# Second sweep: value products of four batches at once, with the high and low weight parts stacked in the 128 rows

## The chip, the cores and the metric

The kernel runs on one core of a Trainium2 chip. Five engines work on it, each through its own queue in program order: TensorE (PE, with its weight loads as PEld), VectorE (DVE), ScalarE (ACT), GpSimd (POOL) and SyncE (SP), which issues all DMAs. The metric is the device time of one execution in microseconds. For the kernel before there are three timed runs, 905.22, 906.84 and 908.5 us, with a median of 906.84.

## The reference

Per batch (8) and head (8), with a sequence of 576, a head size of 64 and 32 memory slots:

```python
a = exp(phi - max_s(phi)); a = a / (sum_s(a) + 1e-09)
k_m = einsum('bhsm,bhsd->bhmd', a, k)
v_m = einsum('bhsm,bhsd->bhmd', a, v)
attn = softmax(q @ k_m.T / 8)            # 576 x 32
x = attn @ v_m                           # heads side by side: 4608 x 512
xn = x / sqrt(mean(x*x) + 1e-06) * rms_g
g = xn @ w_gate; val = xn @ w_val        # 512 -> 1536
out = (silu(g) * val) @ w_out            # 1536 -> 512
```

All data is float32. x is never needed as such: attn @ v_m @ W equals attn @ (v_m W), and v_m has only 32 rows per head. The kernel multiplies the small v_m with a slice of the weights first (the "value product") and attn with that result afterwards.

## The kernel before, in words

**Precision.** The large products run in the faster fp32r format. Each float32 operand is split into a high part (a cast to fp32r, on ACT) and a low part (the remainder, by a subtraction on POOL or DVE). A product is high x high + high x low + low x high, so three matmuls.

**Two sweeps.** The eight batches are four pairs. The first part (up to about 150 us) makes k_m and v_m of all batches and the attention of pairs 0 and 1. Then 48 steps follow: steps 0 to 23 are the first sweep, for pairs 0 and 1, steps 24 to 47 the second, for pairs 2 and 3. The 1536 columns are 12 slices of 128; a step is one pair with one slice. Function `where` gives the order: pair A with slices 0 and 1, pair B with slices 0 and 1, and so on. During the first sweep the attention of pairs 2 and 3 is made on the side, and the weights are converted, split and stored in DRAM (`w_dram`, `o_dram`); the second sweep reloads them (`reload`, L439). Slice numbers 12 to 23 are the second sweep's.

**One step.** `vw_steps` makes the value product: `vp`, two halves cc of six matmuls with 256 columns (L854). The 128 rows that are summed over are the 64 dimensions of two heads; the stationary operand `vm` holds those two heads' memory slots in blocks with zeros between them, which were put there when v_m was transposed, for both batches of the pair. The three matmuls per group are (vh, wh), (vh, wl), (vl, wh). `evac` copies the result to `xh` (ACT cast, L867) and `xl` (DVE, L868), 64 rows at a time. `gv_steps` multiplies these with the attention, `ath` and `atl`, into gate and value, `pg` and `pv` (L892), 48 matmuls of 256 or 320 columns, applies silu (ACT, L900) and the product `hf` (DVE, L901), and splits it into `hh` and `hl` (L914, L915). After two steps of a pair, `out_steps` multiplies both with `w_out` (`oh`, `ol`) into `po`, nine tiles of six 512-wide matmuls (L934), and adds them to `acc` (DVE, L942). The last one of a pair writes `acc` to the output (L946, two DMAs of 64 rows per tile).

**The second sweep's values.** `late_vm` (called at the times LV) reloads the value tiles of pairs 2 and 3 from `vg_dram` and splits them, one pair after the other, into the two `vm` buffers.

**What sets the order.** Every piece is entered in a list with a time in units of steps (the table PRM: GV, VW, O, LV, PSW and others). The list is sorted and a scheduler, which simulates the engines, fixes each engine's queue from it. Tiles rotate through a fixed number of buffers per tag, and a writer waits until the old tile's readers are done. PSUM has one buffer for the value product, two each for gate, value and `o`.

Of the kernel before, what the change touches and what calls it, by code (L numbers as in the profile page):

```python
# [8 lines left out]
F32 = mybir.dt.float32  # L9
F32R = mybir.dt.float32r  # L10
# [9 lines left out]
WB = 4  # L20
# [48 lines left out]
    XN=[0.012, 0.176, 0.184, 0.33, 0.33, 0.566, 0.596, 0.699, 0.766],  # L69
    LV=[22.571, 24.198],  # L70
    CB=1,
# [20 lines left out]
def kernel(  # L92
# [43 lines left out]
    make_identity(nc, ident)  # L136
    vm = {}
    gram = {}
# [16 lines left out]
    def split_v(b, vg):  # L155
        pr, j = divmod(b, 2)
        for e in range(2):
            o = e ^ j
            src = vg.rearrange("p (c e) m -> p c e m", e=2)[:, :, o, :]
            hi, lo = vm[pr][:, 0, :, e, o, :], vm[pr][:, 1, :, e, o, :]  # L160
            nc.scalar.copy(hi, src)
            nc.gpsimd.tensor_tensor(out=lo, in0=src, in1=hi.bitcast(F32), op=ALU.subtract)
# [179 lines left out]
    def convert(kind, n):  # L342
# [99 lines left out]
    with ExitStack() as c1:  # L442
# [133 lines left out]
        def kv_steps(b):  # L576
# [59 lines left out]
            def post2():  # L636
                tp = st.pop(("kvt", b))
                km = km_late.get(b)
                if km is None:
                    km = sb.tile([P, HP, 64], F32, tag="km", name=f"km{b}", bufs=4)  # L640
                nc.scalar.copy(km, tp[:, 0])
                st["km", b] = km
                vt = sb.tile([P, HP, 64], F32, tag="vt", name=f"vt{b}")
                nc.scalar.copy(vt, tp[:, 1])
# [184 lines left out]
    NS = (NP // G) * NU * G * 2  # L829
    vw, hsplit, accs = {}, {}, {}  # L830

    def where(i):

        ps_, r = divmod(i, NU * G * 2)
        u, r = divmod(r, G * 2)
        pi, f = divmod(r, 2)
        return ps_, u, ps_ * G + pi, 2 * u + f

    def vw_steps(i):
# [3 lines left out]
        def mm(cc):  # L843
            def f():
                if cc == 0:
                    vw[i] = [ps.tile([P, 2, 2, 256], F32, tag="vw", name=f"vp{i}", bufs=1)]
                vp = vw[i][0]
                vh, vl = vm[pr][:, 0], vm[pr][:, 1]
# [11 lines left out]
        def evac():  # L860
            vp = vw[i][0]
            xh = sb.tile([P, 2, 2, 256], F32R, tag="xh", name=f"xh{i}", bufs=2)
            xl = sb.tile([P, 2, 2, 256], F32R, tag="xl", name=f"xl{i}", bufs=2)
            for h in range(2):
# [5 lines left out]
                ).ins)  # L870
            vw[i] = xh, xl
        return [mm(0), mm(1), evac]

    def gv_steps(i):
        ps_, u, pr, j = where(i)
        steps = []
        for gi, (t0, n) in enumerate(GROUPS):
            N = 64 * n
            for b in range(2):
                def f(gi=gi, t0=t0, n=n, N=N, b=b):  # L880
# [7 lines left out]
                    for half, pt in ((0, pg), (1, pv)):  # L888
                        m = 0
                        for l, r in ((xh, ah), (xh, al), (xl, ah)):  # L890
                            for cc in range(2):
                                nc.tensor.matmul(  # L892
                                    pt[:, :N],
                                    l[:, cc, b, half * P:half * P + P],
                                    r[:, b, cc, t0:t0 + n, :].rearrange("p t x -> p (t x)"),
# [12 lines left out]

            def split(gi=gi, n=n):
                hf = hsplit[i, gi][0]  # L910
                hh = sb.tile([P, n, P], F32R, tag=f"hh{gi}", name=f"hh{i}_{gi}", bufs=3)
                hl = sb.tile([P, n, P], F32R, tag=f"hl{gi}", name=f"hl{i}_{gi}", bufs=3)
                hv = hf.rearrange("p t b x -> p t (b x)")
# [6 lines left out]
    def out_steps(i):  # L920
# [34 lines left out]

    def late_vm(pr):
        new_vm(pr)
        vg = sb.tile([P, 2, HP, 64], F32, tag="vgl", name=f"vgl{pr}")
        for j in range(2):
            nc.sync.dma_start(vg[:, j], vg_dram[2 * pr + j])  # L960
            split_v(2 * pr + j, vg[:, j])

# [97 lines left out]
    for i in range(NS):  # L1060
        ps_, u, pr, j = where(i)
        ev += place(i, PRM["GV"], gv_steps(i))
        if i + 1 < NS:
# [9 lines left out]
    items, again = [x for x in items if x[1] < NJ], [x for x in items if x[1] >= NJ]  # L1073
    for kind, n, p, e in again:
        if kind != 1:
            ev.append((e, lambda kind=kind, n=n: reload(kind, n)))
    for a, (kind, n, p, e) in enumerate(items):
# [8 lines left out]
    for a in range(NP - G):  # L1086
# [3 lines left out]
        ev += place(PRM["XM"][a], PRM["XN"], steps[n:])  # L1090
        ev.append((PRM["LV"][a], lambda a=a: late_vm(G + a)))
    for _, f in sorted(ev, key=lambda e: e[0]):
# [31 lines left out]
```

## Time and profile before

| | |
|---|---|
| timed runs, median (lowest, highest) | 906.84 us (905.22, 908.5) |
| profiled execution, first to last instruction (span) | 901.6 us |
| PE busy | 838.0 us, 93% of the span |
| DVE, ACT, POOL busy | 573.3, 420.6, 328.0 us |
| mean granted TensorE clock | 0.970 |
| DMA queue of SP | 81432 packets, 105.41 MB, 37.5% of 16 engines |
| matmuls | 6207 |

The profile gives the execution's span and no separate time for it; it is set against the timed median, 5.2 us longer. A row of the page's group list names the line, engine, operation, output and inputs, shapes and count, then busy time and the mean of one, then idle time of the engine before them and what ended it. Matmuls overlap, so their mean duration is longer than the distance between two. In a timeline row the first number is the start, the second the time from there to the end of the merged instructions. "SPq" is SP's DMA queue.

### The profile page before, as it was taken

To read this page: it belongs to the slowest core of one execution; us is meant where nothing else is said; L and a number is where in the kernel's file an instruction comes from. 1 tells how busy PE (TensorE), PEld (TensorE's weight loads), DVE (VectorE), ACT (ScalarE), POOL (GpSimd) and SP (SyncE) were. 2 spreads that over 40 slices of the span, in tenths; PEclk is the share of its full clock that TensorE was granted. 3 is DMA by queue.
4 is the path that set the end of the run, shared out by engine and by line. 5 is a ranking of instruction groups with operands and counts; after the bars stand their busy time and mean duration, and the time that the engine had idled before them with its cause. 6 is when DMAs were issued, how large, how long until landed. Compare 5 with 4: busy or idle time off the path is not lost.

```text
span 901.6 us, 15803 instructions
## 1 busy us (share of the span) xinstructions
PE 838.0 (93%) x6207; PEld 744.9 (83%) x6207; DVE 573.3 (64%) x994; ACT 420.6 (47%) x717; POOL 328.0 (36%) x274
## 2 busy tenths in 40 slices
PE   4999487999998999998999999899999999999997
PEld 4777476888887898987888897898899999999996
DVE  5578956877569878787877746522445455454543
ACT  2657334777745655655544532344423333333330
POOL 3564735563634543633533531411212111121120
PEclk9889787999999999999999999999999999999999
DMA  8976554354325433443333343501204012040046
GB/s 285 341 250 232 202 167 128 108 164 121 126 68 157 148 96 104 151 135 113 128 105 110 103 109 106 129 9 53 88 1 141 1 48 94 1 141 1 1 115 142
DMA packets 81506, 106.41 MB, mean 118 GB/s; under 512 B 34324, under 2 KB 52248, under 8 KB 81432
## 3 DMA queue, kind: packets, MB, share of 16 engines
q1 hardware_dynamic: 81432, 105.41, 37.5%
q8 instruction: 49, 0.80, 0.4%
q14 instruction: 25, 0.20, 0.1%
HBM read 73.93 MB, written 31.46 MB: 117 GB/s over the span
## 4 chain that ended last, share of the span: by engine, by line
PE 70%; DVE 13%; issue 5%; DMA 5%; POOL 3%; ACT 3%; SPq 1%; POOLq 0%; DVEq 0%; ACTq 0%
PE po L934 28%; PE pv L892 14%; PE pg L892 13%; PE vp L854 7%; PE kvp L587 3%; DMA phi<-in_phi_dram 2%; DVE xl L868 1%; POOL w L399 1%; DMA kv<-in_v_dram 1%; DVE ex L353 1%; DVE acc L942 1%; PE xp L236 1%; POOL hl L915 1%; ACT xh L867 1%; PE S L1000 1%
## 5 line engine op out<-in xcount | busy, mean ns | idle before, releaser
L915 POOL TENSOR_TENSOR hl<-hf,hh 128x512 fp32r<-128x512 f32 (+1 forms) x96 | 140.3, 1462 | 356.0 <-ACT hh L914 348.3
L942 DVE TENSOR_TENSOR acc<-po,acc 128x512 f32<-128x512 f32 x180 | 122.4, 686 | 111.2 <-PE po L934 110.3
L934 PE MATMUL po<-oh,hh 128*128 128x512 f32 x432 | 173.3, 402 | 6.9 <-DMA oh<-od 1.6
L934 PE MATMUL po<-oh,hl 128*128 128x512 f32 x432 | 171.4, 397 | 0.0
L934 PE MATMUL po<-ol,hh 128*128 128x512 f32 x432 | 171.1, 396 | 0.0
L868 DVE TENSOR_TENSOR xl<-vp,xh 64x1024 fp32r<-64x1024 f32 x96 | 117.1, 1220 | 55.6 <-ACT xh L867 54.4
L900 ACT ACTIVATE sg<-pg 128x256 f32<-128x256 f32 x192 | 77.2, 409 | 141.4 <-PE pg L892 138.0
L901 DVE TENSOR_TENSOR hf<-pv,sg 128x256 f32<-128x256 f32 x192 | 85.5, 452 | 79.2 <-PE pv L892 51.5
L867 ACT CAST xh<-vp 64x1024 fp32r<-64x1024 f32 x96 | 96.7, 1008 | 51.7 <-PE vp L854 36.0
L914 ACT CAST hh<-hf 128x512 fp32r<-128x512 f32 (+1 forms) x96 | 64.6, 673 | 82.8 <-DVE hf L901 69.9
L934 PEld LDWEIGHTS po<-oh,hh 128*128 128x128 f32 x432 | 81.7, 190 | 21.5 <-DVE acc L942 2.3
L934 PEld LDWEIGHTS po<-oh,hl 128*128 128x128 f32 x432 | 81.7, 189 | 19.6
L934 PEld LDWEIGHTS po<-ol,hh 128*128 128x128 f32 x432 | 81.8, 189 | 11.4
L892 PE MATMUL pg<-ath,xh 128*128 128x320 f32 (+1 forms) x384 | 86.3, 300 | 4.8 <-ACT xh L867 3.6
L854 PE MATMUL vp<-wh,vm 128*128 128x256 f32 x384 | 85.2, 289 | 3.8 <-DVE xl L868 1.7
L892 PE MATMUL pv<-ath,xh 128*128 128x320 f32 (+1 forms) x384 | 85.0, 298 | 0.7 <-DVE hf L901 0.7
L892 PE MATMUL pv<-atl,xh 128*128 128x320 f32 (+1 forms) x384 | 84.8, 296 | 0.0
L892 PE MATMUL pg<-ath,xl 128*128 128x320 f32 (+1 forms) x384 | 84.6, 295 | 0.0
L892 PE MATMUL pg<-atl,xh 128*128 128x320 f32 (+1 forms) x384 | 84.5, 296 | 0.0
L892 PE MATMUL pv<-ath,xl 128*128 128x320 f32 (+1 forms) x384 | 83.0, 295 | 0.0
L892 PEld LDWEIGHTS pg<-ath,xh 128*128 128x128 f32 x384 | 63.5, 189 | 10.6 <-ACT xh L867 4.5
L854 PEld LDWEIGHTS vp<-wh,vm 128*128 128x128 f32 x384 | 65.9, 193 | 7.5 <-ACT wh L416 1.8
(129 smaller groups left out, 1395.2 us busy)
## 6 DMA issues: line engine op xcount, KB each, us to landing
kv<-in_k_dram SPq DMA_DIRECT2D x32, 288.0 KB, 4.7
kv<-in_v_dram SPq DMA_DIRECT2D x32, 288.0 KB, 5.8
out_dram<-acc SPq DMA_DIRECT2D x72, 128.0 KB, 2.4
raw<-in_moe_w_gate_dram SPq DMA_DIRECT2D x12, 512.0 KB, 4.0
raw<-in_moe_w_val_dram SPq DMA_DIRECT2D x12, 512.0 KB, 4.2
wd<-wh SPq DMA_DIRECT2D x12, 512.0 KB, 3.4
wd<-wl SPq DMA_DIRECT2D x12, 512.0 KB, 3.4
raw<-in_moe_w_out_dram SPq DMA_DIRECT2D x12, 512.0 KB, 3.8
```

What stands on the lines that cost most here:

```text
L236: nc.tensor.matmul(xp[64 * j:64 * j + 64, P * cc:P * cc + P], st["at"][:, t, cc, 64 * j:64 * j + 64], gb[:, j, cc], start=True, stop=True,)
L587: nc.tensor.matmul(kvp[64 * par:64 * par + 64, cc, 0:128], e_bd[j][:, hp, c, :], st["kv", b, hp][:, :, 64 * c:64 * c + 64], start=(c == 0) ...
L854: nc.tensor.matmul(vp[:, cc, e, :], lhs(l), r[:, 2 * cc + e, :], start=(n == 0), stop=(n == 2),)
L867: nc.scalar.copy(xh[rows], src)
L868: urgent.append(nc.vector.tensor_tensor(out=xl[rows], in0=src, in1=xh[rows].bitcast(F32), op=ALU.subtract).ins)
L892: nc.tensor.matmul(pt[:, :N], l[:, cc, b, half * P:half * P + P], r[:, b, cc, t0:t0 + n, :].rearrange("p t x -> p (t x)"), start=(m == 0), ...
L900: nc.scalar.activation(sg[:, :N], pg[:, :N], AF.Silu)
L901: urgent.append(nc.vector.tensor_tensor(out=hf[:, :, b, :], in0=pv[:, :N].rearrange("p (t x) -> p t x", x=64), in1=sg[:, :N].rearrange("p ...
L914: nc.scalar.copy(hh, hv)
L915: nc.gpsimd.tensor_tensor(out=hl, in0=hv, in1=hh.bitcast(F32), op=ALU.subtract)
L934: nc.tensor.matmul(po, l[:, tt, :], r, start=(m == 0), stop=(m == 5))
L942: nc.vector.tensor_tensor(out=accs[key], in0=po, in1=accs[key], op=ALU.add).ins
```

## The change

Only the second sweep's value products change, and what feeds them.

- *Rows.* The stored weights are laid out so that, for one head, rows 0 to 63 are one part (high or low) of its 64 rows and rows 64 to 127 the other (the first sweep writes them with four DMAs of 64 rows per slice, before two of 128).
- *Values.* Two tiles `va0` (high) and `va1` (low) take the place of the two pairs' `vm` buffers. Each holds the values of all four batches, once in rows 0 to 63 and once in rows 64 to 127, so that 128 columns are 4 batches x 32 slots of one head. They are fetched by 16 DMAs of 64 rows (`fetch_v`, in the order already at the start of the first sweep), before 4 of 128 rows, and split by `late_v`.
- *Products.* `unit_steps(n)`: for one slice and one head two matmuls, va0 and va1 against the stacked weights, which give all four products of parts. A slice has 8 heads, so 16 matmuls, which serve both pairs.
- *Placing.* The product has its rows in order of batch, the gate products need them in order of head for one batch. ACT and DVE copy the product into staging tiles `sh` (high) and `sl` (low), in buffers that the weight conversion used before. DMAs from SBUF to SBUF, 32 rows each, then put the pieces into `xh` and `xl` of the two steps: 16 for a step, 32 for a slice. The order of heads in the values is permuted (`spread_v`, and `put` in the first part) so that each piece stays in its rows.
- *Order.* From step 28 on the pairs alternate at every step (`mixed`), output groups come after the third and fourth of four steps, and a fourth pair of `hh`/`hl` buffers (`hx`) is added; every third step's `xh`/`xl` are four smaller tiles in another tag. The times U, RL, RW and LV are new.

```diff
-    LV=[22.571, 24.198],
+    LV=[21.0, 21.1, 22.22, 22.25],
+    U=[
+        [-1.6, -1.45, -1.4, -1.25, -0.99, -0.7],
+        [-1.6, -1.5, -1.3, -1.2, -0.99, -0.98],
+        [-1.6, -1.5, -1.3, -1.2, -0.99, 0.01],
+    ],
+    RL=[-2.85, -3.4, -3.3],
+    RW=[1.73, 1.6],
...
+    def spread_v(b, vg):
+        j, pi = b % 2, swapped(b)
+        for h in range(2):
+            x = 4 * h + (h ^ pi)
+            src = vg[:, h].rearrange("p (c e) m -> p c e m", e=2)
+            if j:
+                src = src[:, :, ::-1]
+            places = slice(x + 2, x + 9, 6) if j else slice(x, x + 11, 10)
+            hi, lo = (t[:, :, places, :] for t in vall)
             nc.scalar.copy(hi, src)
             nc.gpsimd.tensor_tensor(out=lo, in0=src, in1=hi.bitcast(F32), op=ALU.subtract)
...
                 for a, t in enumerate(wsplit[n]):
-                    nc.sync.dma_start(w_dram[n][:, a], t.bitcast(F32))
+                    for h in range(2):
+                        r = 64 * (h ^ a)
+                        nc.sync.dma_start(w_dram[n][r:r + 64, h], t[64 * h:64 * h + 64].bitcast(F32))
...
+    def mixed(i):
+        return i >= NS // 2 + 2 * G
...
+        if mixed(i):
+            pi, f = f, pi
...
+    def slot(i):
+        if i >= NS // 2 and i % 3 == 2:
+            t = [[sb.tile([P, 2, 256], F32R, tag="w2", name=f"{x}{i}_{c}", bufs=WB) for c in range(2)] for x in ("xh", "xl")]
+        else:
+            whole[i] = [sb.tile([P, 2, 2, 256], F32R, tag=x, name=f"{x}{i}", bufs=2) for x in ("xh", "xl")]
+            t = [[x[:, c] for c in range(2)] for x in whole[i]]
...
+    def unit_steps(n):
...
+        def mm(cc):
+            def f():
+                st[cc] = vp = ps.tile([P, 2, 2, 256], F32, tag="vw", name=f"vq{n}_{cc}", bufs=1)
+                for e in range(2):
+                    for h in range(2):
+                        k = 8 * e + 4 * h
+                        w = wsplit[n][h][:, 2 * cc + e].rearrange("p g f -> p (g f)")
+                        for a in range(2):
+                            nc.tensor.matmul(
+                                vp[:, h, e, :], vall[a][:, cc, k:k + 4, :].rearrange("p q m -> p (q m)"), w,
+                                start=(a == 0), stop=(a == 1),
+                            )
...
+                for h in range(2):
+                    src = st[cc][:, h]
+                    xh, xl = (x[h][cc] for x in st["x"])
+                    nc.scalar.copy(xh, src)
+                    urgent.append(nc.vector.tensor_tensor(
+                        out=xl, in0=src, in1=xh.bitcast(F32), op=ALU.subtract
+                    ).ins)
...
+        def send(pi):
+            def f():
+                i = steps[pi]
+                slot(i)
+                for a in range(2):
+                    for g in range(4):
+                        rows = slice(32 * g, 32 * g + 32)
+                        for c in range(2):
+                            x = st["x"][a][(g & 1) ^ pi][c][rows].bitcast(F32)
+                            nc.sync.dma_start(vw[i][a][c][rows].bitcast(F32), x[:, ::-1] if g >> 1 else x)
+            return f
+        return [mm(0), take(0), mm(1), take(1), send(0), send(1)]
...
-                for s in (i - 1, i):
+                for s in (i - 2 if mixed(i) else i - 1, i):
...
-        if i % 2:
+        if i % 4 > 1 if mixed(i) else i % 2:
             ev += place(i + 1, PRM["O"], out_steps(i))
+    for n in range(NJ, 2 * NJ):
+        late_n = min(n - NJ, 2)
+        ev += place(steps_of(n)[0], PRM["U"][late_n], unit_steps(n))
+        ev.append((2 * n + PRM["RL"][late_n], lambda n=n: reload(0, n)))
+        ev.append((2 * (n - n % 2) + PRM["RW"][late_n > 1] + 0.1 * (n % 2), lambda n=n: reload(2, n)))
```

More of the change, by code (lines that the diff above doesn't have):

```diff
@@ L640, in post2, with put @@
                     km = sb.tile([P, HP, 64], F32, tag="km", name=f"km{b}", bufs=4)
-                nc.scalar.copy(km, tp[:, 0])
+                def put(dst, src):
+                    if swapped(b):
+                        dst, src = (x.rearrange("p s (h m) -> p s h m", h=2) for x in (dst, src))
+                        src = src[:, :, ::-1]
+                    nc.scalar.copy(dst, src)
+                put(km, tp[:, 0])
                 st["km", b] = km
                 vt = sb.tile([P, HP, 64], F32, tag="vt", name=f"vt{b}")
-                nc.scalar.copy(vt, tp[:, 1])
+                put(vt, tp[:, 1])
                 st["vt", b] = vt, tp
@@ new lines, in steps_of, with take, f @@
+    def steps_of(n):
+        return [i for i in range(NS) if where(i)[0] * NJ + where(i)[3] == n]
+    def unit_steps(n):
+        steps = steps_of(n)
+        st = {}
+        def mm(cc):
[11 more added lines that the diff above has]
+            return f
+        def take(cc):
+            def f():
+                if cc == 0:
+                    high = [wp[0].tile([P, 2, 2, 256], F32R, tag="raw", name=f"sh{n}_{h}", bufs=2) for h in range(2)]
+                    st["x"] = [[[x[:, c] for c in range(2)] for x in high], [[], []]]
+                for h, (pool, tag) in enumerate(((wp[0], "mi"), (sb, "vgl")) if cc else ((wp[0], "ex"), (wp[0], "w"))):
+                    st["x"][1][h].append(pool.tile([P, 2, 256], F32R, tag=tag, name=f"sl{n}_{h}{cc}"))
+                for h in range(2):
[5 more added lines that the diff above has]
+                    ).ins)
+            return f
+        def send(pi):
+            def f():
+                i = steps[pi]
[6 more added lines that the diff above has]
+                            nc.sync.dma_start(vw[i][a][c][rows].bitcast(F32), x[:, ::-1] if g >> 1 else x)
+            return f
+        return [mm(0), take(0), mm(1), take(1), send(0), send(1)]
@@ L907, in gv_steps, with split @@
                 steps.append(f)
-            def split(gi=gi, n=n):
+            def split(gi=gi, t0=t0, n=n):
                 hf = hsplit[i, gi][0]
-                hh = sb.tile([P, n, P], F32R, tag=f"hh{gi}", name=f"hh{i}_{gi}", bufs=3)
-                hl = sb.tile([P, n, P], F32R, tag=f"hl{gi}", name=f"hl{i}_{gi}", bufs=3)
+                if mixed(i) and i % 4 == 3:
+                    if gi == 0:
+                        fourth.append(persist.tile([P, 2, NT, P], F32R, tag="at", name=f"hx{i}"))
+                    hh, hl = (fourth[-1][:, a, t0:t0 + n] for a in range(2))
+                else:
+                    hh = sb.tile([P, n, P], F32R, tag=f"hh{gi}", name=f"hh{i}_{gi}", bufs=3)
+                    hl = sb.tile([P, n, P], F32R, tag=f"hl{gi}", name=f"hl{i}_{gi}", bufs=3)
                 hv = hf.rearrange("p t b x -> p t (b x)")
@@ L954, in o_tile, with fetch_v, late_v @@
         return ps.tile([P, 512], F32, tag="o", name=name)
[L956 to L961, printed above, removed]
+    late = {}
+    def fetch_v(pr):
+        pool, tag = ((sb, "vgl"), (wp[0], "w"))[pr - G]
+        late[pr] = both = pool.tile([P, 2, 2, HP, 32], F32, tag=tag, name=f"vgl{pr}")
+        for k in range(2):
+            b = 2 * pr + k
+            for h in range(2):
+                x = 32 * (h ^ swapped(b))
+                for r in range(2):
+                    nc.sync.dma_start(
+                        both[64 * r:64 * r + 64, k, h], vg_dram[b][64 * h:64 * h + 64, :, x:x + 32]
+                    )
+    def late_v(pr):
+        if not vall:
+            vall[:] = [persist.tile([P, 2, 16, 32], F32R, tag=f"vm{a}", name=f"va{a}") for a in range(2)]
+        both = late.pop(pr)
+        for k in range(2):
+            spread_v(2 * pr + k, both[:, k])
     def attend_steps(pr, s):
@@ L1072 @@
                 items.append((kind, n, 2 * n0 + PRM["PRE" if n0 else "PRE0"][a], 2 * n0 + PRM["PSW"][a]))
[L1073 to L1076, printed above, removed]
+    items = [x for x in items if x[1] < NJ]
     for a, (kind, n, p, e) in enumerate(items):
@@ L1090 @@
         ev += place(PRM["XM"][a], PRM["XN"], steps[n:])
-        ev.append((PRM["LV"][a], lambda a=a: late_vm(G + a)))
+        for p, f in zip(PRM["LV"][a::2], (fetch_v, late_v)):
+            ev.append((p, lambda a=a, f=f: f(G + a)))
     for _, f in sorted(ev, key=lambda e: e[0]):
```

24 lines of the change are left out of this document (14 added, 10 removed).

## The prediction

> **What bounds the kernel now.** I read the totals by engine first, then the stretch of the second sweep in one row, then what TensorE (PE) waits for from 500 us on.
>
> ```profile
> PE 838.0 (93%) x6207; PEld 744.9 (83%) x6207; DVE 573.3 (64%) x994; ACT 420.6 (47%) x717; POOL 328.0 (36%) x274
> core 0: us, PE busy (x) PEld busy (x) DVE busy (x) ACT busy (x) POOL busy (x), PEclk, DMA share, GB/s
> 650.00:850.00 200.00, 200.00 (x1237) 182.21 (x1235) 102.66 (x150) 68.70 (x113) 40.09 (x28) 1.00 0.15 48
> PE rp L205 <- DVE rinv L277: 2.3, 1, 2.3
> PE po L934 <- DMA oh<-od: 1.6, 1, 1.6
> ```
>
> PE is busy for 200 of 200 us, at a granted clock of 1.00, while VectorE (DVE) is half idle and the DMA engines are used at 0.15. After 500 us only two PE waits exceed a microsecond. So here a matmul less is time less, and new time can only come from a wait put in front of PE. The mean of one matmul on the page overlaps its neighbours; the price is the distance between starts:
>
> ```profile
> 713.20 0.46 PE L892 MATMUL pv<-atl,xh 128*128 128x320 f32 x2
> 713.49 0.46 PE L892 MATMUL pv<-ath,xl 128*128 128x320 f32 x2
> 713.78 0.28 PE L854 MATMUL vp<-wh,vm 128*128 128x256 f32 x1
> 713.90 0.29 PE L854 MATMUL vp<-wl,vm 128*128 128x256 f32 x1
> 714.03 0.40 PE L854 MATMUL vp<-wh,vm 128*128 128x256 f32 x2
> 714.27 0.28 PE L854 MATMUL vp<-wl,vm 128*128 128x256 f32 x1
> 714.38 0.28 PE L854 MATMUL vp<-wh,vm 128*128 128x256 f32 x1
> 714.50 0.46 PE L892 MATMUL pg<-ath,xh 128*128 128x320 f32 x2
> 694.12 1.87 PE po L934 x8
> 709.97 1.41 PE po L934 x6
> 750.29 1.87 PE po L934 x8
> ```
>
> Six product matmuls take 714.50 - 713.78 = 0.72 us, 0.12 each; a 320-wide one 0.147 (0.29 for two); a 512-wide one 1.87 / 8 = 0.234. From 694.12 to 750.29 the program repeats itself after four steps, 14.04 us a step.
>
> **Fewer matmuls.** Before, a half of a step's product is six matmuls for one pair of batches:
>
> ```order
> L854 MATMUL vp36_7818<-wh18_7709,vm2_5938 128x256
> L854 MATMUL vp36_7818<-wl18_7710,vm2_5938 128x256
> L854 MATMUL vp36_7818<-wh18_7709,vm2_5938 128x256 x2
> L854 MATMUL vp36_7818<-wl18_7710,vm2_5938 128x256
> L854 MATMUL vp36_7818<-wh18_7709,vm2_5938 128x256
> ```
>
> Now, at the same place on PE, a half is eight, and serves both pairs (vq18 stands for weight slice 18, va0 and va1 for the high and low part of all four batches' values):
>
> ```order
> L898 MATMUL vq18_1_8024<-wh18_7755,va0_5922 128x256
> L898 MATMUL vq18_1_8024<-wh18_7755,va1_5923 128x256
> L898 MATMUL vq18_1_8024<-wl18_7756,va0_5922 128x256
> L898 MATMUL vq18_1_8024<-wl18_7756,va1_5923 128x256
> L898 MATMUL vq18_1_8024<-wh18_7755,va0_5922 128x256
> L898 MATMUL vq18_1_8024<-wh18_7755,va1_5923 128x256
> L898 MATMUL vq18_1_8024<-wl18_7756,va0_5922 128x256
> L898 MATMUL vq18_1_8024<-wl18_7756,va1_5923 128x256
> ```
>
> Per slice that is 16 for 24; over 12 slices 96 matmuls fewer, of the same size: **-96 x 0.12 = -11.5 us**. A slice's two steps go from 28.1 to 27.1 us.
>
> **Evacuation.** Two casts and two subtractions of 64x1024 per step become, per slice, four and four of 128x512.
>
> ```profile
> 710.45 0.62 ACT L914 CAST hh<-hf 128x512 fp32r<-128x512 f32 x1 [1.31 <-DVE hf L901]
> 706.62 1.01 ACT L867 CAST xh<-vp 64x1024 fp32r<-64x1024 f32 x1 [1.01 <-DVE xl L868]
> 711.42 0.69 DVE L942 TENSOR_TENSOR acc<-po,acc 128x512 f32<-128x512 f32 x1 [1.05 <-PE po L934]
> 708.68 1.23 DVE L868 TENSOR_TENSOR xl<-vp,xh 64x1024 fp32r<-64x1024 f32 x1
> ```
>
> By the nearest rows ScalarE (ACT) saves 0.4 and DVE 0.5 us each time. Neither is what PE waits for, so this counts 0.
>
> **The sends** are the new thing between a product and its reader: 32 DMAs of 32 rows (64 KB) per slice, all on SP's queue, 384 in all. The nearest rows are the output writes (64 rows, 128 KB, in a burst at the end) and the od reload:
>
> ```profile
> L946 SPq DMA_DIRECT2D out_dram<-acc x28: 466/594/1347, 875.0 to 898.2; - x28
> DMA to landing us min/median/max: 2.2/2.4/3.6
> 880.38 18.45 SPq L946 DMA_DIRECT2D out_dram<-acc x24
> 743.68 0.86 SPq L439 DMA_DIRECT2D oh<-od x2
> ```
>
> A send should cost SP between 0.43 (0.86 / 2) and 0.59 us; half of them read one run per row and half two, so I take 0.49. Landing: 2.4 us. A slice then takes SP 32 x 0.49 + 4 reloads x 0.43 = 17.4 of 27.1 us: the queue has room, and what counts is the lead. I added up PE's new order at the prices above, from a slice's last product to the first read of what its second half sends, and against it set the first cast (0.62), k sends and a landing. Slice 15: lead 9.8 us, need 0.62 + 8 x 0.49 + 2.4 = 6.9. Slice 18: 9.3 against 7.4 (k = 9). Slice 20: 10.5 against 6.9. The others have more. Slice 13, the second at the transition, has not:
>
> ```order
> L1043 DMA out_0_dram<-acc0_8_2449 64x512 x2
> L929 DMA xh25_6370<-sh13_1_6259 32x512
> L929 DMA xh25_6370<-sh13_0_6258 32x512
> L929 DMA xh25_6370<-sh13_0_6258 32x2x256
> L929 DMA xh25_6370<-sh13_1_6259 32x512
> L929 DMA xh25_6370<-sh13_0_6258 32x2x256
> L929 DMA xh25_6370<-sh13_1_6259 32x2x256 x2
> ```
>
> That is SP (step 25's high part xh25, from the staging tiles sh13); before, only the output writes stood here. Its first-half rows come mixed with second-half ones, behind two output writes. On PE between vq13's end and the first read of xh25:
>
> ```order
> L207 MATMUL tp3_6_6288<-ident_58,ain3_4_6107 128x128 x4
> L258 MATMUL xp3_6_6322<-gb_63,at3_6077 64x128 x4
> L258 MATMUL xp3_7_6351<-gb_63,at3_6077 64x128 x4
> L207 MATMUL tp3_8_6356<-ident_58,ain3_8_6132 128x128 x2
> L258 MATMUL xp3_8_6365<-gb_63,at3_6077 64x128 x4
> L1031 MATMUL po23_0_6426<-oh10_5828,hh22_0_5957 128x512
> ```
>
> Eighteen small matmuls and one output group of six. Before, these transposes and xp products of pair 3 were spread among step 25's gate products; now they stand ahead of them.
>
> ```profile
> 544.19 0.66 PE L236 MATMUL xp<-gb,at 128*64 128x128 f32 x8
> 544.78 0.66 PE L185 MATMUL tp<-ident,ain 128*128 128x128 f32 x4
> ```
>
> Small ones cost (544.78 - 544.19) / 8 = 0.074: 18 x 0.074 + 1.4 = 2.7 us of cover. Needed: 0.62 + 5 x 0.49 + 2.4 = 5.4. **+2.7 us**, once. The other slices: nothing at these prices, and with 3.6 us of landing (the longest output write) 18 still has 0.7 left. Sixteen landings per step now stand as waits before PE where one or two did; the reloaded oh, which also waits for landings, costs no gap at 694.12 (eight at 0.234). I put **+2.0** for queueing on ACT, DVE and SP that this addition leaves out (bounds 0 and 9, below).
>
> **Waits that go.** Both PE waits quoted at the start stand at places that the order changes; the second is this row:
>
> ```profile
> 638.45 0.49 PE L934 MATMUL po<-oh,hh 128*128 128x512 f32 x1 [1.62 <-DMA oh<-od]
> ```
>
> The first: rp waited 2.3 us for rinv after the last xp of pair 3. Between the two PE now has 1.4 us more work and the 2.7 us wait: **-2.3**. The 1.6 us for oh fell where the order left 3.6 us between the last use of the old and the first of the new slice; the shortest such gap is now 4.5: **-1.6** (0 if the sends ahead delay the reload).
>
> **Values.** The tiles for four batches can be filled only when vp23 has read the old ones; vq12 follows 8.6 us of PE work later.
>
> ```profile
> L161 ACT CAST vm<-vgl x8: 294/298/301, 475.6 to 496.5; 128x128 fp32r<-128x128 f32 x8
> L162 POOL TENSOR_TENSOR vm<-vgl,vm x8: 451/464/467, 475.9 to 497.5; 128x128 fp32r<-128x128 f32 x8
> 154.35 0.38 SPq L330 DMA_DIRECT2D raw<-in_moe_w_gate_dram  x1
> 165.69 0.38 SPq L330 DMA_DIRECT2D raw<-in_moe_w_val_dram  x1
> ```
>
> Eight casts and subtractions, as before, need 0.3 + 8 x 0.46 = 4.0 us: 0 (about 3 if GpSimd (POOL) is held that long). Their 16 fetches for 4, and the 24 extra writes of the weights lie in the first sweep, at 150 us mostly between these two loads, 11 us apart: 0, or 12 x 0.49 = 6 us of a late load if that slack is not there. Alternating pairs moves the output groups, none added; PE has them between the gate products as before: 0.
>
> **Sum:** -11.5 + 2.7 + 2.0 - 2.3 - 1.6 = -10.7. The profiled span is 901.6, the runs' median 906.84: 5.2 us lie around it. Span 890.9, time **896.1 us**.
>
> **Rivals.** (a) *Landings later under the sends' own traffic*, at 4.5 us instead of 2.4: slice 13 pays 2.1 more, 18 pays 0.2, and what stands behind them on ACT and DVE some 3: -10.7 + 5.3 = -5.4, **901.4**.  Against it: DMA share 0.15. (b) *The waits eat the gain*, 0.9 us at each of 12 slices: **907**, no change. (c) *SP becomes the bound.* The order gives each DMA a wait on the one eight before it.
>
> ```profile
> kv<-in_v_dram SPq DMA_DIRECT2D x32, 288.0 KB, 5.8
> SPq L299 <- DMA kv<-in_v_dram: 1.9, 4, 0.7
> ```
>
> That wait shows only in the crowded opening, where landing is 5.8. At 5.8 a send costs 5.8 / 8 = 0.73: 32 x 0.73 + 1.7 = 25 of 27.1 us, and a slice needs 0.62 + 8 x 0.73 + 5.8 = 12.3 against leads near 10: some 2.3 us at eleven slices and 4.6 more at slice 13, -10.7 + 30 = +19: **926**, slower. It decides from about 1.1 us per slice on (-10.7 + 12 x 1.1 = +2.5), a landing near 5. For it: one queue, many small transfers. Against: 24 writes of 128 KB left in 18.45 us at 2.4. (d) *Sends go one after another*, 32 x 2.4 = 77 us per slice against 27: 12 x 50 = 600 us more. Against: 24 x 2.2 / 18.45 = 2.9 in flight in the tail. [...] (e) *The change doesn't reach the steps it names*: the order has 192 vq where 288 vp stood, so it does.
>
> **Chances.** Forecast 58% (its own range 893 to 900); more hidden than that 6%; (a) 15%; (b) 9%; (c) 10% and (d) 2%. Under 0.3% (2.7 us) a measurement of this kernel can't tell a change from none: faster 0.79, same 0.09, slower 0.12. The range 892.5 to 906 leaves out most of (b), (c), (d) and a little below.
>
> **What would show it.** 192 vq groups at 0.12 each and no L854 rows after 570 us; PE busy over 99% between 650 and 840; one PE wait of 2 to 3 us on a DMA into xh near 565; rp without its wait; sends at 0.43 to 0.59 us with landing near 2.4. Landing above 4.5, or PE waits on DMA at every slice, would prove me wrong.

## The result, and the profile after

The changed kernel takes 896.55 us (median of six runs, 893.85 to 899.57) where the kernel before, run beside it, takes 905.46 (904.74 to 908.5): a ratio of 0.990, with an interval of 0.9875 to 0.9924. The forecast was 896.1. Two later sets of five runs of the changed kernel gave 893.34 and 895.69 us, ratios of 0.9875 (0.9858 to 0.9892) and 0.988 (0.9861 to 0.9896).

The totals by engine on the page of the changed kernel:

```profile
PE 825.7 (92%) x6111; PEld 732.6 (82%) x6111; DVE 546.3 (61%) x994; ACT 399.3 (45%) x717; POOL 328.3 (37%) x274
```

The stretch of the second sweep that was shown of before, in the same columns:

```profile
650.00:850.00 200.00, 198.79 (x1205) 179.92 (x1205) 88.09 (x152) 57.79 (x115) 41.73 (x29) 1.00 0.50 129
```

PE has 96 matmuls less and is still busy for 198.79 of 200 us; DVE has fallen from 102.66 to 88.09 and ACT from 68.70 to 57.79; the DMA engines are used at 0.50 where it was 0.15, and move 129 GB/s where it was 48. A half of a value product now looks like this on PE's timeline:

```profile
744.48 0.28 PE L898 MATMUL vq<-wh,va 128*128 128x256 f32 x1
744.59 0.40 PE L898 MATMUL vq<-wl,va 128*128 128x256 f32 x2
744.83 0.40 PE L898 MATMUL vq<-wh,va 128*128 128x256 f32 x2
745.07 0.40 PE L898 MATMUL vq<-wl,va 128*128 128x256 f32 x2
```

And the sends in the view of their line, with the issue time in ns as minimum, median and maximum, then first and last start:

```profile
L929 SPq DMA_DIRECT2D xh<-sh x192: 525/595/1767, 512.4 to 843.3; - x192
L929 SPq DMA_DIRECT2D xl<-sl x192: 512/594/1704, 518.3 to 848.5; - x192
DMA to landing us min/median/max: 1.9/2.0/8.0
```

A matmul costs (745.07 - 744.59) / 4 = 0.12 us, as before. A send takes SP 0.595 us and lands in 2.0.

**Which part of the program got shorter.** The spans are 901.6 and 893.7 us, 7.9 apart, but the two executions already stand apart before the second sweep begins. Up to a group of xp products near 480 us PE has the same instructions in the same order in both. It begins here before:

```profile
477.56 0.66 PE L236 MATMUL xp<-gb,at 128*64 128x128 f32 x8
```

and here in the changed kernel, where the next group follows at once:

```profile
480.93 1.29 PE L258 MATMUL xp<-gb,at 128*64 128x128 f32 x16
```

I call this instruction the marker. From it to the end of the span are 901.6 - 477.56 = 424.0 us before and 893.7 - 480.93 = 412.8 after, **11.3 less**, against 3.4 lost ahead of it. Whether those 3.4 belong to the change is the first thing that the experiments had to settle.

What PE waits for in the changed kernel from 480 us on, grouped by line (us in total, times, longest; the rows left out come to 1.0 us):

```profile
PE xp L258 <- ACT at L217: 1.6, 2, 1.4
PE po L1031 <- DMA oh<-od: 1.2, 2, 0.8
PE xp L258 <- DVE acc L1039: 1.1, 1, 1.1
PE tp L207 <- DVE ssq L271: 0.7, 2, 0.5
PE xp L258 <- DVE at L217: 0.5, 1, 0.5
```

There is no wait on a send. The 2.3 us of rp for rinv are gone and a new one, in the chain of pair 3's transposes and xp products, has come. The window from the marker to PE's last matmul, before and then after:

```profile
477.56:896.79 419.23, 412.96 (x2552) 370.66 (x2552) 213.53 (x353) 150.52 (x257) 98.97 (x77) 1.00 0.25 72
480.93:888.83 407.90, 401.62 (x2456) 358.88 (x2456) 186.35 (x353) 129.14 (x254) 101.01 (x80) 1.00 0.53 135
```

PE stands idle for 6.3 us in both, so in these two profiles the waits cancel and the 11.3 us are PE's busy time. Each of the two also holds one short stretch of a lower granted clock. Before, it follows the wait of rp, here in windows of 5 us (the last three columns are clock, DMA share and GB/s):

```profile
565.00:570.00 5.00, 2.74 (x12) 2.25 (x11) 3.48 (x13) 0.00 (x0) 0.09 (x1) 0.77 0.46 105
570.00:575.00 5.00, 5.00 (x32) 4.45 (x31) 2.66 (x4) 1.48 (x4) 2.54 (x2) 0.89 0.24 55
```

In the changed kernel it follows the new wait and is shown in the last section. In windows of 1 us such a stretch is a clock of 0.50 for a little over 3 us; the busy time in these windows, times the clock that is missing, gives an estimate of 1.7 us for either kernel, so these cancel too.

### The profile page after: what moved, and what is told of

It is laid out like the page before. It is cut to its first block, busy times and chain, and to the rows that moved or that the text cites. A ratio compares the mean times of both kernels' runs of the same rounds, so it can differ in the third digit from the quotient of the medians.

```text
span 893.7 us, 16377 instructions
## 1 busy us (share of the span) xinstructions
PE 825.7 (92%) x6111; PEld 732.6 (82%) x6111; DVE 546.3 (61%) x994; ACT 399.3 (45%) x717; POOL 328.3 (37%) x274
## 4 chain that ended last, share of the span: by engine, by line
PE 68%; DVE 10%; DMA 7%; issue 6%; ACT 4%; POOL 3%; SPq 2%; DVEq 0%; POOLq 0%; ACTq 0%
PE po L1031 29%; PE pv L984 13%; PE pg L984 13%; PE vp L948 3%; PE vq L898 2%; PE kvp L611 2%; DMA phi<-in_phi_dram 2%; PE xp L258 1%; DMA oh<-od 1%; DMA q<-in_q_dram 1%; DVE ex L375 1%; DVE xl L961 1%; SPq L929 1%; POOL w L421 1%; DVE acc L1039 1%
## 5 line engine op out<-in xcount | busy, mean ns | idle before, releaser
L1012 POOL TENSOR_TENSOR hl<-hf,hh 128x512 fp32r<-128x512 f32 (+1 forms) x86 | 126.3, 1469 | 299.1 <-ACT hh L1011 274.0
L1031 PE MATMUL po<-oh,hh 128*128 128x512 f32 x387 | 155.8, 404 | 6.5 <-DVE ex L1122 1.5
L1031 PE MATMUL po<-ol,hh 128*128 128x512 f32 x387 | 153.4, 396 | 0.5 <-DMA ol<-od 0.5
L1031 PE MATMUL po<-oh,hl 128*128 128x512 f32 x387 | 153.5, 397 | 0.0
L1031 PEld LDWEIGHTS po<-oh,hh 128*128 128x128 f32 x387 | 73.1, 189 | 19.8 <-issue 2.5
L1031 PEld LDWEIGHTS po<-oh,hl 128*128 128x128 f32 x387 | 73.2, 189 | 17.4
L984 PEld LDWEIGHTS pg<-ath,xh 128*128 128x128 f32 x384 | 64.1, 189 | 11.2 <-ACT xh L960 4.7
L421 POOL TENSOR_TENSOR w<-mi,ex 128x512 f32<-128x512 f32 x34 | 43.9, 1291 | 71.9 <-ACT mi L412 52.6
L961 DVE TENSOR_TENSOR xl<-vp,xh 64x1024 fp32r<-64x1024 f32 x48 | 58.5, 1219 | 18.1 <-ACT xh L960 17.4
L984 PEld LDWEIGHTS pv<-ath,xh 128*128 128x128 f32 x384 | 64.7, 190 | 4.7 <-DVE hf L993 0.7
L984 PEld LDWEIGHTS pv<-ath,xl 128*128 128x128 f32 x384 | 63.0, 188 | 2.0 <-issue 0.2
```

Source lines behind the costliest of these rows:

```text
L421: (nc.gpsimd if on_pool else V).tensor_tensor(out=d["w"], in0=m, in1=ex, op=ALU.mult)
L961: urgent.append(nc.vector.tensor_tensor(out=xl[rows], in0=src, in1=xh[rows].bitcast(F32), op=ALU.subtract).ins)
L984: nc.tensor.matmul(pt[:, :N], l[cc][:, b, half * P:half * P + P], r[:, b, cc, t0:t0 + n, :].rearrange("p t x -> p (t x)"), start=(m == 0), ...
L1012: nc.gpsimd.tensor_tensor(out=hl, in0=hv, in1=hh.bitcast(F32), op=ALU.subtract)
L1031: nc.tensor.matmul(po, l[:, tt, :], r, start=(m == 0), stop=(m == 5))
```

## Experiments

**1. The kernel before once more.** No edit.

> The kernel before, unchanged, for a second profile. In the profile of the changed kernel the first 130 us, whose instructions stand in the same order in both, end 3.4 us later than in the profile of before. If that is scatter between executions (theory), this second profile of before differs from the first by some microseconds there too, and from about 170 us on keeps that shift. If the change's copies of the last two batches (read in swapped halves) cost those 3.4 us (rival), the two profiles of before agree within 1 us.

Its marker stands at 481.39 us and its span is 905.0, so 423.6 us from the marker to the end. The opening was 3.8 us longer than in the first profile of the very same program. In the changed kernel's three profiles the marker stands at 480.93, 480.09 and 481.01 us. Over all thirteen profiles of this case it lies between 477.6 and 483.5 us. The opening scatters by some 4 to 6 us from one execution to the next; the 3.4 us are no effect of the change, and what the change does is read from the marker on.

**2. The third product left out of the kernel before.**

```diff
-                    for n, (l, r) in enumerate(((vh, wh), (vh, wl), (vl, wh))):
+                    terms = ((vh, wh), (vh, wl), (vl, wh))[:2 if ps_ else 3]
+                    for n, (l, r) in enumerate(terms):
...
-                            start=(n == 0), stop=(n == 2),
+                            start=(n == 0), stop=(n == len(terms) - 1),
```

> The kernel before, with the third matmul of each product group left out in the second sweep (low values times high weights are not added; 96 matmuls of 256 columns less, nothing else changed, no sends). Theory (a matmul less is 0.12 us less, sends and waits of the change are nothing in sum): -11.5 us, the same as or up to 3 us better than the changed kernel. Rival (the change's sends cost several us that something else pays back): better than the changed kernel by 4 us or more. Rival (off the path): no change.

**3. The matmuls put back into the changed kernel.**

```diff
-                        for a in range(2):
+                        for a, first, last in ((0, True, True), (0, True, False), (1, False, True)):
...
-                                start=(a == 0), stop=(a == 1),
+                                start=first, stop=last,
```

> The changed kernel with a throwaway matmul ahead of each group of two, so that a slice has 24 again; all sends stay, the sum is unchanged. Theory: 96 x 0.12 = 11.5 us more than the changed kernel, that is 0 to +3 us against before. Rival (PE has room because it waits for sends anyway): less than half of the 11.5 us shows.

**4. The changed kernel once more**, beside these two.

> The changed kernel, unchanged, for a tighter ratio and a second profile. Theory (scatter in the opening, -11.3 us in the second sweep): the opening's shift against before lies anywhere between -1 and +4 us, and from the last common instruction to the end it takes 412 to 414 us, as in the first profile (412.8). Rival (the opening is really slower): +3 to +4 us again.

| kernel | runs' median (us) | ratio to before, interval | marker to end (us) |
|---|---|---|---|
| before, two profiles | 905.46, 905.62 | | 424.0, 423.6 |
| changed, three profiles | 896.55, 893.34, 895.69 | 0.990, 0.9875, 0.988 | 412.8, 415.1, 409.3 |
| before without the third product | 892.81 | 0.987 (0.9852 to 0.9882) | 412.4 |
| changed, 24 matmuls per slice again | 904.59 | 1.000 (0.9984 to 1.0013) | 424.1 |

Taking 96 matmuls out of the kernel before, with nothing else changed, gives what the whole change gives: 423.8 - 412.4 = 11.4 us. Putting 96 matmuls back into the changed kernel takes it all away: 424.1 against a mean of 412.4. Per matmul that is 0.119 us. One profile of a kernel can lie some 3 us from the next (412.8, 415.1 and 409.3 for the changed one), so the medians of the runs on one chip are the firmer figures: 905.62 - 892.81 = 12.8 us for the matmuls taken out, 904.59 - 893.34 = 11.3 for those put back. And the kernel before without them lies 0.5 us under the changed one (892.81 and 893.34), with intervals that overlap. So 384 sends, alternating pairs, placed rows and permuted values cost PE together nothing that these runs can see. In the second profile of the changed kernel, 415.1 us where 412 to 414 were expected, a wait of 1.1 us for reloaded weights (wl) is new. In experiment 3 one wait on a send did appear, at slice 14, where this order leaves no matmul between the product and its reader:

```profile
PE pg L984 <- DMA xh<-sh: 3.5, 1, 3.5
```

A second stretch of low clock follows it there (0.80 in the window from 595 to 600 us), while the waits for oh and for an addition of DVE are missing: PE's idle time is 6.1 us in all, near the 6.3 of before. That the waits come out even is chance.

**5. How much lead the sends need: products half a step later.**

```diff
-        [-1.6, -1.5, -1.3, -1.2, -0.99, 0.01],
+        [-1.1, -1.0, -0.8, -0.7, -0.49, 0.51],
```

> The changed kernel with the value products of slices 14 to 23 half a step (about 7 us) later, so that the lead of the sends falls to 6 to 10 us (slices 16, 18, 21: 6.2 to 6.8 us). My theory (384 sends cost PE nothing because the lead covers 0.62 us of cast, 8 issues of 0.6 and 2.0 us of landing, 7.4 us in all): PE waits on sends of about 1 us each at slices 16, 18 and 21 and none elsewhere, from the marker to the end 413 to 418 us, ratio 0.988 to 0.994. The rival that SP's queue is close to its bound: waits at most slices that add up, over 430 us and a ratio over 1.005. If the lead does not matter at all (sends issued long before): as the changed kernel, no wait on a send.

894.74 us, ratio 0.990 (0.988 to 0.992), 412.6 us from the marker: no loss, and no wait on a send anywhere; waits for reloaded weights, 1.5 us in all, are new against the first profile, and the stretch of low clock is missing (1.00 in every window of 20 us from 480 to 880). My count of 7.4 us of need was too high. The place with the shortest lead is slice 18. PE's timeline there, from the end of the product to the first gate product that reads what was sent last:

```profile
705.20 0.40 PE L898 MATMUL vq<-wl,va 128*128 128x256 f32 x2
711.70 0.28 PE L984 MATMUL pg<-ath,xh 128*128 128x256 f32 x1
```

and SP's:

```profile
704.02 5.15 SPq L929 DMA_DIRECT2D xh<-sh  x8
```

The product ends near 705.6. By then SP is already issuing: it issues eight sends of xh from 704.02 to 709.17, since the first half of the columns was cast before and could go ahead. So 3.6 us of issue lie behind the product and not 4.8, the cast is hidden under them, and the read comes 2.5 us after the last issue, a little over one landing. 6.1 us of lead were enough.

**6. Without alternating pairs.**

```diff
     def mixed(i):
-        return i >= NS // 2 + 2 * G
+        return False
```

> The changed kernel without the alternation of the pairs: two steps of one pair, then two of the other, as in the kernel before, everything else as it is. The odd slices' xh is then read 0 to 4 us after the product in the order (slices 16, 18, 20: 1.5, 3.4 and 0 us of lead; 22: 0). Theory: each of these waits for what is missing to about 7.4 us: 5.9 + 4 + 7.4 + 7.4 = 25 us at most, so 431 to 438 us from the marker to the end and 910 to 922 us, the gain gone. Rival, the alternation is only there for the output groups and costs or brings nothing: 893 to 898 us.

906.69 us, ratio 1.002 (0.9997 to 1.0035): the gain is gone. From the marker 424.0 us, 11.2 more than the changed kernel. The longest of PE's waits that the changed kernel lacks:

```profile
PE pg L984 <- DMA xh<-sh: 2.1, 3, 1.7
PE pg L984 <- issue: 1.3, 1, 1.3
PE pg L984 <- DMA xl<-sl: 0.9, 2, 0.7
```

The window from the marker to PE's last matmul in the changed kernel, and then here:

```profile
480.93:888.39 407.46, 401.19 (x2455) 358.87 (x2456) 186.35 (x353) 129.14 (x254) 101.01 (x80) 1.00 0.53 135
```

```profile
479.29:898.24 418.95, 404.81 (x2455) 359.78 (x2456) 186.25 (x353) 127.66 (x254) 100.97 (x80) 1.00 0.52 131
```

The same 2455 matmuls stand in 418.95 us for 407.46; PE is idle for 418.95 - 404.81 = 14.1 us for 6.3, and the rest of the 11 us is longer busy time (404.81 for 401.19). The wait put down to "issue" stands before the first product that reads xl at 628.87 us; the weight load in front of it waited 1.5 us for a send of xl, so it is one of the sends' too. That makes 4.3 us of the 7.9 more that PE is idle. The others are waits for ACT, DVE and reloads that come with the other order, and for the longer busy time I have no cause: the granted clock falls once, as in the first profile of the changed kernel (0.50 for some 3 us behind that wait of 1.3 us). The direction is the theory's, the size is not: I had expected up to 25 us, because I took the first gate product of a step to need all of xh. The waits of at most 1.7 us fit a need of one half of the columns and one batch, with the others following as they land; no run tests this by itself. So without the alternation the time is up by as much as the 96 matmuls bring, but the sends' waits are only part of it.

**7. Where SP's room ends: each send cut in two.**

```diff
-                    for g in range(4):
-                        rows = slice(32 * g, 32 * g + 32)
+                    for g in range(8):
+                        rows = slice(16 * g, 16 * g + 16)
...
-                            x = st["x"][a][(g & 1) ^ pi][c][rows].bitcast(F32)
-                            nc.sync.dma_start(vw[i][a][c][rows].bitcast(F32), x[:, ::-1] if g >> 1 else x)
+                            x = st["x"][a][(g >> 1 & 1) ^ pi][c][rows].bitcast(F32)
+                            nc.sync.dma_start(vw[i][a][c][rows].bitcast(F32), x[:, ::-1] if g >> 2 else x)
```

> The changed kernel with each send cut into two of 16 rows: 64 sends of 32 KB per slice for 32 of 64 KB, the same bytes. Theory: what a send costs is its issue on SP, 0.6 us whatever its size, so that SP needs 64 x 0.6 + 1.7 = 40 of 27 us per slice and becomes the bound: about 13 us more per slice over 10 to 12 slices, 1020 to 1060 us in all, with PE waits on sends at every slice. Rival, the issue goes with the bytes (0.3 us for half of them): SP needs 21 us as now and the time stays within 893 to 900 us. A landing much over 2.0 us would say that the transfers, not the issue, are what crowds.

One execution: 1109.75 us. The view of the sends' line:

```profile
L929 SPq DMA_DIRECT2D xh<-sh x384: 507/591/1762, 512.3 to 1068.2; - x192
DMA to landing us min/median/max: 1.9/2.0/7.6
```

What PE waits for, and behind it the window from the marker to PE's last matmul:

```profile
PE pg L984 <- DMA xl<-sl: 101.7, 19, 8.2
PE pg L984 <- DMA xh<-sh: 36.8, 11, 10.4
```

```profile
480.77:1102.40 621.63, 463.18 (x2455) 404.28 (x2456) 189.38 (x353) 131.55 (x254) 100.44 (x80) 0.85 0.35 89
```

Half the bytes take SP the same 0.59 us to issue, and land in the same 2.0 us. What a send costs here is its issue, the same at both sizes; the rival that issue goes with the bytes falls. With twice as many, SP is the bound, and 30 waits on sends take 138.5 us of PE. The time is above my 1020 to 1060 for two reasons: the sends come 0.635 us apart and not 0.6 (10.17 us for 16), which with the reloads and with some 2 us in which SP itself waits makes a slice 45 us and not 40; and PE, idle a quarter of the time, ran at a mean clock of 0.85. So rival (c) of the prediction is real, with its price on the issue and not on the landing, and the change stands at a distance of it: with 32 sends SP issues for 154 of the 190 us between 650 and 840.

**8. Pair 3's chain spread.** The wait that had come new was to be taken away.

```diff
-    XS=[0.1086, 0.0359],
-    XM=[21.887, 24.858],
+    XS=[0.1086, 0.06],
+    XM=[21.887, 25.35],
```

> The changed kernel with pair 3's transposes and xp products spread again over the transition (their spacing 0.06 steps for 0.0359, and their start half a step later). In the changed kernel PE waits some 4 us in their chain and runs at a clock of 0.77 for some 2.5 us after it. Theory: that wait goes and with it about 1 us of slow clock, while the wait of rp for rinv (2.3 us before) or of the first read of xh25 for its sends (up to 2.7 us) may come back: from the marker to the end 408 to 412 us, 2 to 4 us less than the changed kernel, ratio 0.983 to 0.986. Rival, one wait takes the other's place in full: as the changed kernel, 412 to 415 us and a ratio of 0.987 to 0.990.

897.52 us, ratio 0.993 (0.9907 to 0.9957), 415.7 us from the marker: nothing gained, and its ratio is above those of the changed kernel. Waits in the chain of xp fell to some 2 us, but another came, for reloaded weights. On PE's timeline:

```profile
580.53 0.79 PE L898 MATMUL vq<-wh,va 128*128 128x256 f32 x2 [2.56 <-DMA wh<-wd]
```

On SP's:

```profile
568.86 5.10 SPq L1043 DMA_DIRECT2D out_dram<-acc  x8
574.00 1.88 SPq L463 DMA_DIRECT2D wh<-wd  x1
```

And the window from 580 us on:

```profile
580.00:585.00 5.00, 4.47 (x17) 4.48 (x18) 0.49 (x1) 0.82 (x2) 0.26 (x1) 0.50 0.94 300
```

The weights of slice 14 are reloaded behind 16 sends and eight output writes in SP's queue; PE now came to them earlier and waited 2.56 us. In the window from 580 us the granted clock is 0.50 and PE does 17 matmuls. The rival was right: one wait took the other's place. PE's idle time is 7.0 us for 6.3 in the first profile of the changed kernel; the rest of the loss is busy time, with a clock of 0.50 for twice as long.

**9. One output DMA for two.** In the changed kernel SP issues with hardly a pause through this whole transition: 67 sends, 36 output writes, 8 reloads and two writes of weights between 512 and 590 us.

```diff
-                    for b in range(2):
-                        nc.sync.dma_start(
-                            out[(2 * pr + b) * S:(2 * pr + b + 1) * S].rearrange("(p c) d -> p c d", c=NT)[:, t, :],
-                            accs[key][64 * b:64 * b + 64, :],
-                        )
+                    rows = out[2 * pr * S:(2 * pr + 2) * S].rearrange("(p c) d -> p c d", c=NT)[:, t, :]
+                    if pr < G:
+                        nc.sync.dma_start(rows, accs[key])
+                    else:
+                        for b in range(2):
+                            nc.sync.dma_start(rows[64 * b:64 * b + 64], accs[key][64 * b:64 * b + 64, :])
```

> The changed kernel with one output DMA of 128 rows for two of 64 in the first sweep's pairs, so 18 DMAs fewer for SP between 525 and 585 us. In the changed kernel SP issues there without a pause (64 sends, 36 output writes, 8 reloads in 56 us), and the reload of slice 14's weights comes out only at 575 us. Theory (SP's issue time is the tightest resource at the transition and only there, and the changed kernel's PE just escapes it): SP is free 18 x 0.6 = 11 us earlier, the reload comes out near 566 us, PE waits on reloads of about 1 us go; from the marker to the end 411 to 413 us, 0 to 2 us less than the changed kernel. Rival, one DMA of 128 rows takes SP twice as long as one of 64: nothing moves, 412 to 415 us.

**10. Both edits.**

> Both edits: pair 3's xp chain spread, and one output DMA of 128 rows for two of 64 in the first sweep's pairs. Spreading the chain alone brought nothing: PE reached slice 14's products about 2 us earlier and waited 2.6 us for their weights, whose reload stood behind the output writes in SP's queue, and then ran at half clock for some 3 us. Theory: with 18 DMAs fewer ahead of it the reload is there, so this wait and the slow clock go and the spread chain's gain shows: from the marker to the end 408 to 411 us, ratio 0.981 to 0.985. Rival, something else is late next (the first read of xh25 or xh28 for its sends, whose lead is 2.7 and 3.1 us with the spread chain): 412 to 416 us, ratio 0.986 to 0.993.

**11. The changed kernel beside them.**

> The changed kernel unchanged, on the same chip as the two runs beside it, since these differ from it by less than one per cent: from the marker to the end 412 to 416 us, ratio 0.987 to 0.990, and the stretch of slow clock after the gaps of the xp chain as before if it belongs to the program and not to the run.

| kernel, same chip | runs' median (us) | ratio to before, interval | marker to end (us) |
|---|---|---|---|
| changed | 895.69 | 0.988 (0.9861 to 0.9896) | 409.3 |
| one output DMA for two | 890.52 | 0.983 (0.9811 to 0.9849) | 407.5 |
| that and pair 3's chain spread | 894.39 | 0.986 (0.9840 to 0.9888) | 411.3 |

One output DMA for two makes 5 us in the medians, with intervals apart: of all versions run it is the fastest, 1.7% under the kernel before. SP's timeline shows the reload of slice 14's weights where it was expected (first the changed kernel's first profile, then this one):

```profile
570.07 5.03 SPq L1043 DMA_DIRECT2D out_dram<-acc  x8
575.14 1.41 SPq L463 DMA_DIRECT2D wh<-wd  x1
```

```profile
563.89 2.48 SPq L1044 DMA_DIRECT2D out_dram<-acc  x4
566.42 0.45 SPq L463 DMA_DIRECT2D wh<-wd  x1
```

The view of its output line, and behind it the two longest of PE's waits after the marker:

```profile
L1044 SPq DMA_DIRECT2D out_dram<-acc x18: 332/528/1325, 520.3 to 580.0; - x18
```

```profile
PE xp L258 <- DVE at L217: 0.8, 1, 0.8
PE po L1031 <- DMA oh<-od: 0.5, 1, 0.5
```

A DMA of 128 rows takes SP 0.53 us, one of 64 rows 0.55 (the median in the changed kernel): the rival that it takes twice as long falls, as for the sends. From the marker 407.5 us is 1.8 under the third profile of the changed kernel, about what the waits there (4.8 us in all) lose against these (2.7); neither has a stretch of low clock (1.00 in every window of 5 us from 500 to 600). Against the mean of the three profiles, 412.4, it is 4.9 less, and it lies below the 411 to 413 I gave. But the scheduler, which knows of the freed queue, also set the pieces of pair 3 otherwise on PE, so how much is the earlier reload and how much the new order isn't told apart. With the chain spread on top, the wait for slice 14's weights fell to 0.8 us as expected, and 2.0 us of waiting for an addition of DVE came in the chain; 411.3 us is outside the 408 to 411 I gave, the ratio of 0.986 is the rival's, and the low clock came once more, at 545 us (0.66 in the window from there to 550). Spreading that chain is not the improvement I took it for. The changed kernel's third profile is, at 409.3 us, below the 412 to 416 I gave: the low clock that I had counted on did not come.

## Why the prediction was right, point by point

**-11.5 for 96 matmuls: right.** Experiments 2 and 3 measure 11.4 and 11.7 us in the profiles, 12.8 and 11.3 in the medians, from both sides.

**+2.7 for slice 13: the wait did not come.** The step that failed is the cover of 2.7 us. PE's timeline of the changed kernel from the product on:

```profile
548.92 0.40 PE L898 MATMUL vq<-wl,va 128*128 128x256 f32 x2
551.11 1.09 PE L258 MATMUL xp<-gb,at 128*64 128x128 f32 x16 [1.35 <-ACT at L217]
552.72 0.44 PE L207 MATMUL tp<-ident,ain 128*128 128x128 f32 x2 [0.52 <-DVE ssq L271]
553.67 0.98 PE L258 MATMUL xp<-gb,at 128*64 128x128 f32 x8 [0.52 <-DVE at L217]
557.30 0.28 PE L984 MATMUL pg<-ath,xh 128*128 128x256 f32 x1
```

and SP's:

```profile
549.37 4.72 SPq L929 DMA_DIRECT2D xh<-sh  x7
```

From the product's end near 549.2 to the first read of xh25 at 557.30 are 8.1 us, not 2.7. Sixteen matmuls stand where the order has eight (a row "x4" of xp in the order is eight matmuls in the trace, so I counted half), they wait for ACT and DVE, and the output group behind them ran at a lower clock (0.50 from 554 to 557 us). The sends were issued by 554.1, so the transfers had 3.2 us for a landing of 2.0. In experiment 8 the chain was spread and only 2.7 us stood between product and first read, and again the profile names no wait on a send (0.5 us before the first read of xl25 are put down to nothing). There the half-tile reads of the step are mixed with output groups, and I take the pieces to have landed ahead of each. So the need of 5.4 us, with all eight sends as one block, was too high as well.

**+2.0 for queueing on ACT, DVE and SP at the other slices: near 0.** There is no PE wait on a send in any of the three profiles of the changed kernel; a wait of 1.1 us for reloaded weights, which stand in the same queue, is in one of them.

**-2.3 for rp and rinv: right, but its time went to the next wait.** The wait is gone; 1.6 + 1.1 + 0.7 + 0.5 = 3.9 us of waits stand in the chain of pair 3 ahead of it, at the place where I had put the wait for sends. I had read the order's new block of transposes and xp products as cover, and not asked whether its own inputs are there in time. The sum also put nothing for the clock: before, the output group behind rp's wait ran at 0.50, and in two of three profiles of the changed kernel the one behind the chain did.

**-1.6 for oh: did not come.** In the first two profiles 1.1 to 1.2 us of waits for oh and 0.5 for ol remain, at other slices, in the third 0.3 for oh; before they were 1.6 and, in the second profile, 1.2. So the bound of 0 was about the case. Reloads stand behind sends in SP's queue, which may be why; no run tests it.

**Sends at 0.49 us and a landing of 2.4: 0.595 and 2.0.** One up, one down. SP's load was set too low (17.4 of 27.1 us a slice; measured 154 of 190 us, so 22), which mattered only at the transition, where output writes and reloads come on top. I had put nothing there.

**The sum.** -10.7 was forecast; -11.4 is what the three profiles of the changed kernel have in the mean behind the marker (8.7 to 14.5 one by one), and the medians lie 8.9, 12.3 and 10.0 us under those of before. Of its five terms the first carries all of it, and the other four, +0.8 together, are 0 together, though three of the four are wrong by themselves. That they cancel is luck, and so is a forecast within 0.5 us of a median that itself moves between 893.3 and 896.6. And of the 5.2 us between span and median that I added, an execution itself has 1.7 to 3.2, mostly 1.8 to 2.0 (895.68 us for a span of 893.7); the rest goes with the short opening in the one profile that I had.

**The rivals.** (a) landing at 4.5: no, 2.0. (b) waits that eat the gain: not here, though experiment 6 shows that the order alone decides it. (c) SP as the bound: not at 32 sends, yes at 64. (d) sends one after another: no; eight issued in 5.15 us with 2.0 of landing each have about three in flight (8 x 2.0 / 5.15 = 3.1).

## What to carry to other kernels

Where PE was busy throughout a stretch (198.79 of 200 us), a matmul less was worth its distance in time to the next one (0.12 us in the timeline, 0.119 by experiments 2 and 3), and the extra work on idle engines and queues cost nothing that the runs show as long as the order left a lead (6.1 us at the shortest place of experiment 5); so the order is part of the change, and here taking the alternation out cost as much as the matmuls bring (11.2 and 11.4 us). Count a queue's load in DMAs and not in bytes (a send took SP 0.59 us with 32 KB and with 64), and at the place where most work meets on it, not in the steady state (18 DMAs fewer there, with the order that came with them, made 5 us in the medians). A wait that is taken off PE can uncover the next input that is late (2.56 us for reloaded weights in experiment 8), so before an edit is made for it, look at when that one is there.

## What was not expected of the hardware

**The same gaps cost differently from one execution to the next.** In the chain of pair 3 (544 to 558 us), PE stands still for 3.5 us in the first and in the third profile of the changed kernel, in gaps of at most 1.4. Two windows of the changed kernel's first profile (a clock of 0.77 is a mean of 1.00 and 0.50), and two rows of PE's timeline in the second of them:

```profile
550.00:555.00 5.00, 2.86 (x27) 2.05 (x28) 2.87 (x8) 1.54 (x3) 1.55 (x1) 0.89 0.51 112
555.00:560.00 5.00, 5.00 (x24) 4.16 (x24) 3.03 (x15) 0.00 (x0) 0.00 (x0) 0.77 0.44 99
```

```profile
555.60 0.63 PE L1031 MATMUL po<-oh,hl 128*128 128x512 f32 x1
556.03 0.63 PE L1031 MATMUL po<-oh,hh 128*128 128x512 f32 x1
```

The same windows and rows of its third profile:

```profile
550.00:555.00 5.00, 2.70 (x29) 1.97 (x30) 3.05 (x9) 1.70 (x4) 1.54 (x1) 1.00 0.49 113
555.00:560.00 5.00, 5.00 (x31) 4.41 (x30) 4.03 (x20) 0.00 (x0) 0.00 (x0) 1.00 0.41 92
```

```profile
554.99 0.39 PE L1031 MATMUL po<-oh,hl 128*128 128x512 f32 x1
555.22 0.40 PE L1031 MATMUL po<-oh,hh 128*128 128x512 f32 x1
```

PE stood still for as long in both, but in the first the granted clock fell, matmuls of 512 columns came 0.43 us apart instead of 0.23, and 24 were done where 31 were in the other. The second profile fell too (0.80 and 0.86 in these windows); experiments 5 and 6, with nearly the same gaps there, did not (1.00 in both windows). So the program alone doesn't decide it. The kernel before, with one gap of 2.3 us in front of rp, fell in both its profiles (0.77 from 565 to 570 us in the first, a mean of 0.91 from 560 to 580 us in the second). What decides it, no run shows: gaps of the same size, the longest 1.4 us, came with the lower clock and without it. With the lower clock the first profile has 412.8 us behind the marker and the third, without it, 409.3; of these 3.5 us some 2.2 are busy time (401.19 for 398.95), the rest shorter waits.

**The issue time of a DMA did not go with its size here.** On SP sends of 32 KB and of 64 KB take 0.59 us, and an output of 128 rows 0.53 where 64 rows take 0.55 (medians). Experiment 9 has 18 DMAs fewer and 5 us less in the medians, though the order on PE changed with them. The issue of a send, 0.59 us, stands against a landing of 2.0, and yet in experiment 7 it is the issue that bounds the kernel: the sends come 0.635 us apart, 64 in a slice, and PE waits 138.5 us on them.
